# Delta-rule chunks feeding a softplus FFN on one core: loads, one place's matmuls, an inverse's finish and the weight splits moved

## The chip, the cores and the metric

The program runs on one NeuronCore of a Trainium2 chip. The metric is device time in microseconds of one launch. The kernel before was timed three times: 560.78 us is the median, 558.14 the lowest and 563.43 the highest. One more execution was profiled; the profiler puts it at 561.84 us, of which 560.1 us lie between its first and its last instruction (its span). Differences of this kernel under about 1% are not told from no change by a few runs.

## The reference

Attention with the delta rule runs over 32 heads of 768 tokens and 48 channels, token by token. Its outputs, as 3072 rows of 384, go through a two-layer network with a softplus between the layers.

```python
k_n = k / (norm(k, axis=-1) + 1e-06)
for t in range(S):                                  # S = 768
    y[t] = q[t] @ state
    v_old = k_n[t] @ state
    state = state + beta[t] * outer(k_n[t], v[t] - v_old)
x = y.transpose(0, 2, 1, 3).reshape(B * S, H * D)   # 3072 x 384
h = x @ w_in                                        # 384 -> 2048
g = maximum(h, 0) + log1p(exp(-abs(h)))
out = g @ w_out                                     # 2048 -> 384
```

## The kernel before

The 768 tokens are cut into 12 chunks of 64. In a chunk the recurrence becomes a triangular system, whose matrix comes from the products of the keys among themselves (`gram`, L192) and is inverted for two chunks at a time. `invert(u)` does the pair of chunks 2u and 2u+1: for u = 0 on DVE (VectorE), for u = 1 to 5 on POOL (GpSimd) with the lines L338 and L342 in turn. `finish(u)` turns the inverse round with two DVE transposes (L345, L348), and `scale_v` (L146, DVE) scales the values of the pair's first chunk.

Each chunk's output is a piece of x. The FFN takes it in seven passes: chunk 0, chunk 1, then two chunks at a time. A pass of one chunk has 8 *places*, one of two chunks 16, so there are 96 places, t = 0 to 95. At place t the program writes, in this order: `hidden` of t (TensorE, PE: the first layer, L693, for two tiles f = 2g and 2g+1 of 128 hidden units in the passes of one chunk, where g is t within the pass), its Abs, Exp and Ln on ACT (ScalarE, L698 to L700), a helping of the inverse that is running in the background, the blocks of the recurrence that a table `plan` puts at t, the softplus of t on DVE, the weight splits of `LOWS[t]`, `output` of place t-1 (PE, the second layer, L739), the blocks of t + 0.5, and the weight splits of `HIGHS[t]`. Each engine works its own queue in the order written. A helping is as large as due times and a cost table (`costs`, `room`) make it; `END[u]` is the place at which `finish(u)` and `scale_v` enter the background list, and what is due by a place is run off in it.

The pass of chunk 0 multiplies in plain f32 (two records on PE for a matmul), and its softplus is one DVE instruction (L711). From chunk 1 on values go as a high and a low part, three products each: x as x high and x low, the softplus output as `gh` and `gl` (L705, L707, L708 on DVE), the weights as W[f,0] (made by ACT, L666, the table `HIGHS`) and W[f,1] (made by DVE, L670, in `low(f)`, the table `LOWS`). In a trace W[f,1] is the tile a with number f. Place 8+g is the first that uses tiles 2g and 2g+1, so `low(13)` is needed at place 14, as the third of the nine products of f = 13.

Ahead of place 0 stand the loads (all on the SP queue, in the order written), the products of the keys of chunks 0 to 3, the first inverse on DVE, the products `first_p` (L506), and dummy matmuls (`warm`, L815) that nobody reads. The number of columns is their argument; each is two records. Then come `top` and `expand` (ACT L363 and DVE L365), `couple` (L377), `base` (L395), sweeps, `first_u` (DVE L526, ACT L530 and L531) and `first_y`, whose two ACT copies (L548) are the x of place 0. `convert` (DVE L650) joins the two halves of a weight tile.

Of the kernel before, what the change touches and what calls it, by code (L numbers as in the profile page):

```python
# [19 lines left out]
B, H, S, D = 4, 8, 768, 48  # L20
NT, DM, DFF = B * S, H * D, 2048
P = 128
# [4 lines left out]
NK = DM // P  # L27
# [6 lines left out]
ON_ACT = range(2, NS)  # L34
HIGHS = {3: (0,), 4: (1,), 5: (2,), 6: (3, 4), 7: (5, 6), 8: (7, 8, 9), 9: (10, 11),
         10: (12,), 11: (13,), 12: (14, 15)}
LOWS = {5: (0,), 6: (1, 2), 7: (3,), 8: (4, 5, 6), 9: (7,), 10: (8, 9, 10), 11: (11,), 12: (12, 13), 13: (14, 15)}

PASSES = ((0,), (1,), (2, 3), (4, 5), (6, 7), (8, 9), (10, 11))
ROWS, COLS = [[p for p in PASSES if len(p) == k] for k in (1, 2)]  # L40
PASS = {s: i for i, p in enumerate(PASSES) for s in p}

STEPS = {2: (8, 8.5, 9, 9.5, 10.5, 11, 11), 3: (11.5, 12, 13, 13, 13.5, 14, 14)}
CLEAR, DONE, END, GRAM, INV = {}, {1: 8, 2: 19}, {1: 6, 2: 17}, {4: 3.5, 5: 7}, {2: 11}
CLEAR.update({2: 9, 3: 12})
Q_FIRST = (2, 4, 5, 6, 7, 8, 9, 10)
for c in range(4, NS, 2):
    t, u = 8 * (c - 2) + 3, c // 2
# [12 lines left out]
def deltanet_moe(ctx, tc, kT, qT, kI, vN, beta, wts, out, outT):  # L61
    nc = tc.nc
# [13 lines left out]
    def bank(shape):  # L76
        turns[0] += 1
        if turns[0] % 4 == 0 and not both[0]:
            return ps_o.tile(shape, F32, name="po2")
        return ps_a.tile(shape, F32, name="pa")  # L80
# [9 lines left out]
    def hid(shape):  # L90
        t = lent(shape)
        hids[0] += 1
        return t


    tk = [slice(h * C, (h + 1) * C) for h in range(2)]
# [23 lines left out]
    copies = (nc.scalar.copy, nc.vector.tensor_copy)  # L120
# [3 lines left out]
    def load_k(s):  # L124
        kts[s] = KT[s % 4]
        for ab in range(2):
            nc.sync.dma_start(kts[s][dr[ab]], kT[s, ab])

    def load_beta(u):
        bet[u] = two.tile([P, HB], F32, name="bet")  # L130
        nc.sync.dma_start(bet[u], beta[:, u])

    def load_q(s):
        for ab in range(2):
            nc.sync.dma_start(bv[dr[ab], ab, :, 0:C], qT[s, ab])

    def load_ki(s):
        for ab in range(2):
            nc.sync.dma_start(ki[tk[ab], ab], kI[s, tk[ab]])

    def load_v(s):
        NV[s] = two.tile([P, NP, D], F32, name="nv")
        nc.sync.dma_start(NV[s], vN[s])
# [377 lines left out]
    def first_u(g, to):  # L521

        x = x_base[:, 0, 4 * g:4 * g + 4].rearrange("p (b k) c -> p k b c", k=2)
        for ab in range(2):
            t = tk[ab]
            nc.vector.tensor_tensor(still[t, ab, g, 0:2, :, 0:D], x[t],  # L526
                                    to[0][t].rearrange("p (b k) c -> p k b c", k=2), op=ALU.add)
        u = to[1].rearrange("p (b k) c -> p b k c", k=2)
        for ab in range(2):
            nc.scalar.copy(still[tk[ab], ab, g, 2, :, 0:D], u[tk[1 - ab], :, 0])  # L530
            nc.scalar.copy(still[tk[1 - ab], ab, g, :, :, D:],  # L531
                           u[tk[1 - ab], :, 1].rearrange("p b (k c) -> p k b c", k=NK))

# [98 lines left out]
    def top_half(f):  # L632

        t = tops[f % 2].bitcast(F16).rearrange("p (i n w) -> p i n w", i=2, w=2)
        for i, raw in enumerate((RA[f], RB[f])):
            h = raw.bitcast(BF16).rearrange("p (n w) -> p n w", w=4)
            nc.scalar.copy(t[:, i, :, 1], h[:, :, 2])  # L640

    def convert(n=1, parts=(0, 1)):
        for _ in range(n):
            f = done[0]
            if f == done[1]:
                return
            for i in parts:
                words = (RA[f], RB[f])[i].rearrange("p (n w) -> p n w", w=2)
                h = slice(i * DM, (i + 1) * DM)
                nc.vector.scalar_tensor_tensor(RA[f][:, h], words[:, :, 0], 13, tops[f % 2][:, h],  # L650
                                               op0=ALU.logical_shift_right, op1=ALU.bitwise_or)
            if 1 in parts:
                HF[f] = RA[f].bitcast(F32)
                done[0] = f + 1

    def top(n=1):
        for _ in range(n):
            if done[1] in RB:
                assert done[1] < done[0] + 2
                top_half(done[1])  # L660
                done[1] += 1
# [6 lines left out]
    def low(f):  # L668
        W[f, 1] = one.tile([P, 2 * DM], F32R, name=f"a{f}")
        nc.vector.tensor_tensor(W[f, 1], HF[f], W[f, 0], op=ALU.subtract)  # L670


    n = B * C
    PH, A, G, PO = {}, {}, {}, {}

    def weight(i, f, a, c, n):
        return W[f, a][:, c:c + n] if i else HF[f][:, c:c + n]


    def tiles(i, g):  # L680
        return (2 * g, 2 * g + 1) if len(PASSES[i]) == 1 else (g,)

    def hidden(i, g):
        xr = [[X[i][:, k, m].rearrange("p j b t -> p (j b t)") for k in range(NK)]
              for m in range(2 if i else 1)]
        terms = TERMS if i else TERMS[:1]
        fs = tiles(i, g)
        ph = PH[i, g] = hid([P, len(fs), 2 * n // len(fs)])
        for j, f in enumerate(fs):
            c = 0  # L690
            for k in range(NK):
                for a, b in terms:
                    nc.tensor.matmul(ph[:, j], weight(i, f, a, k * P, P), xr[b][k],  # L693
                                     start=(c == 0), stop=(c == len(terms) * NK - 1))
                    c += 1
        ph = PH[i, g] = ph.rearrange("p f t -> p (f t)")
        a = A[i, g] = two.tile([P, 2 * n], F32, name="a")
        nc.scalar.activation(a, ph, AF.Abs)  # L698
        nc.scalar.activation(a, a, AF.Exp, scale=-1.0)  # L699
        nc.scalar.activation(a, a, AF.Ln, bias=1.0)  # L700
# [59 lines left out]
    def run(g):  # L760
        while True:
            try:
                next(g)
            except StopIteration as e:
                return e.value
# [31 lines left out]
    still = one.tile([P, 2, 2, NK, 2, C], F32, name="ot")  # L797
# [12 lines left out]
    def warm(*columns, behind=None):  # L810

        r = even if behind is None else behind
        to = unread[0] if unread else bank([P, 512])
        for m in columns:
            nc.tensor.matmul(to[:, 0:m], even[:, 0:P], r[:, 0:m], start=True, stop=True)  # L815

    with tc.manual_schedule(engines={ET.PE, ET.DVE, ET.Activation, ET.Pool, ET.SP}):
# [7 lines left out]
            nc.gpsimd.memset(bv[pad[ab], ab, :, 0:C], 0.0)  # L825
        load_q(0)
        load_k(2)
        load_v(0)
        load_ki(0)
        load_k(3)  # L830
        load_beta(1)
        feed(4)
        load_v(1)
# [50 lines left out]
        gram(3)  # L884
        pts.append(first_p(1))
        unread.append(bank([P, 512]))
        warm(512, 512)
        run(iv)
        lq = one.tile([P, 2, NP // 2, C], F32, name="ltq")
        MT[0] = [lq[:, 0], lq[:, 1], two.tile([P, NP // 2, C], F32, name="gh")]  # L890
# [15 lines left out]
        def pairs(g):  # L906
            return [(ps_o, ps_h)[g == 0].tile([P, 4, D], F32, name=f"{'po' if g else 'ph'}{e}")
                    for e in range(2)]

        for g in range(2):  # L910
            i, to = slice(4 * g, 4 * g + 4), pairs(g)
# [4 lines left out]
                nc.gpsimd.tensor_copy(x_base[tk[h], 1, i], x_swap[tk[1 - h], i])  # L916
        rest()
        warm(128)
        top()
        for b in range(C // QB):  # L920
            expand(1, b, nc.scalar)
# [11 lines left out]
        for g in range(2):  # L933
            sweep(0, 2, tos[g], 4 * g, 4, ends=(False, True))
            first_u(g, tos[g])
# [3 lines left out]
        load_q(1)  # L939
        load_k(4)  # L940
        load_v(2)
        convert(1, (1,))
        convert()
        rest_of_u()
        top(2)
# [107 lines left out]
        for c in range(2, NS, 2):  # L1053
            u = c // 2
# [8 lines left out]
            for s in (c, c + 1):  # L1063
                a, b, k0, k1, v, y, z = STEPS[s]
# [29 lines left out]
        for t in range(8 * NS):  # L1094
            costs[t] = costs.get(t, 0) + 960 * len(LOWS.get(t, ()))
            costs[t] += 1700 if t > 7 else 2900 if t < 5 else 700
        for i, p in enumerate(PASSES):
            for g in range(NF // 2 * len(p)):
                t = NF // 2 * p[0] + g
                both[0] = both[0] or t >= FOUR  # L1100
                assert done[0] >= 2 * g + 2 or i
                if t < 8 * NS - 1:
                    hidden(i, g)
                if i == 0:
                    convert(2)
                if t == 8 * NS - 2:
                    hidden(i, g + 1)
                over = min(pull(room(t) + over), 0)
                while background and background[0][2] <= t:
                    run(background.pop(0)[0])  # L1110
                for block in plan.pop(t, ()):
                    block()
                softplus(i, g)
                if i == 0:
                    top(2)
                for f in LOWS.get(t, ()):
                    low(f)
                if late:
                    output(*late)
                for block in plan.pop(t + 0.5, ()):  # L1120
                    block()
                for f in HIGHS.get(t, ()):
                    high(f)
                late = i, g
# [61 lines left out]
```

## Time and profile before

| what | value |
|---|---|
| median of three runs | 560.78 us |
| lowest, highest | 558.14, 563.43 us |
| profiled execution, its span | 561.84 us, 560.1 us |
| mean granted clock of TensorE | 0.996 |
| busy: PE, DVE, ACT, POOL | 541.9, 366.9, 363.5, 203.7 us |

Busy time of an engine is the time in which at least one of its instructions runs. A wait is the stretch in which an engine has nothing running, and it is put down to what released it. Times in the rows are microseconds from the start of the span.

### The profile page before, as it was taken

To read this page: it belongs to the slowest core of one execution; us is meant where nothing else is said; L and a number is where in the kernel's file an instruction comes from. 1 tells how busy PE (TensorE), PEld (TensorE's weight loads), DVE (VectorE), ACT (ScalarE), POOL (GpSimd) and SP (SyncE) were. 2 spreads that over 40 slices of the span, in tenths; PEclk is the share of its full clock that TensorE was granted. 3 is DMA by queue.
4 is the path that set the end of the run, shared out by engine and by line. 5 is a ranking of instruction groups with operands and counts; after the bars stand their busy time and mean duration, and the time that the engine had idled before them with its cause. 6 is when DMAs were issued, how large, how long until landed. Compare 5 with 4: busy or idle time off the path is not lost.

```text
span 560.1 us, 17601 instructions
## 1 busy us (share of the span) xinstructions
PE 541.9 (97%) x7477; PEld 445.5 (80%) x7477; DVE 366.9 (66%) x663; ACT 363.5 (65%) x719; POOL 203.7 (36%) x362
## 2 busy tenths in 40 slices
PE   6879999899999999999999999999999999999997
PEld 4567777698987888878888888888888887888885
DVE  7959976999757857368747378747465736444444
ACT  4668877798677864756774757754567754454453
POOL 7122897129970188701886001886000000000000
PEclk9999999899999999999999999999999999999999
DMA  9909913132130122220122320031220020010001
GB/s 209 332 34 334 362 40 69 35 80 67 57 87 4 38 69 60 78 75 4 32 71 59 71 87 3 9 85 31 58 77 4 1 71 2 14 58 1 1 0 57
DMA packets 35502, 39.56 MB, mean 71 GB/s; under 512 B 22528, under 2 KB 25216, under 8 KB 35424
## 3 DMA queue, kind: packets, MB, share of 16 engines
q1 hardware_dynamic: 35280, 38.18, 23.9%
q8 instruction: 59, 0.97, 0.7%
q10 hardware_dynamic: 144, 0.26, 0.1%
q14 instruction: 19, 0.16, 0.1%
HBM read 31.55 MB, written 4.72 MB: 65 GB/s over the span
## 4 chain that ended last, share of the span: by engine, by line
PE 67%; POOL 14%; DVE 5%; issue 2%; ACT 2%; ACTq 0%; DVEq 0%
PE po L739 29%; PE ph L693 27%; POOL Z L342 7%; POOL tmp L338 7%; PE pa L598 3%; PE pa L481 2%; PE pa L441 2%; PE pa L567 1%; DVE tt L348 1%; PE pa L579 1%; PE ph L579 1%; DVE tt L345 1%; PE ph L241 1%; DVE a L705 1%; DVE Z L326 0%
## 5 line engine op out<-in xcount | busy, mean ns | idle before, releaser
L693 PE MATMUL ph<-x,b 128*128 128x512 f32 (+1 forms) x576 | 166.3, 373 | 0.0
L698 ACT ACTIVATE a<-ph 128x512 f32<-128x512 f32 x96 | 57.4, 598 | 155.1 <-PE ph L693 150.5
L693 PE MATMUL ph<-x,a 128*128 128x512 f32 (+1 forms) x384 | 129.5, 375 | 0.6 <-ACT x L548 0.6
L705 DVE SCALAR_TENSOR_TENSOR a<-ph,a 128x512 f32<-128x512 f32 x88 | 60.6, 688 | 94.2 <-ACT a L700 93.8
L693 PEld LDWEIGHTS ph<-x,b 128*128 128x128 f32 x576 | 105.1, 188 | 19.4
L739 PE MATMUL po<-gh,b 128*128 128x512 f32 (+1 forms) x241 | 97.6, 405 | 1.2 <-DVE gh L707 1.2
L342 POOL TENSOR_TENSOR Z<-Z,tmp 128x30 f32<-128x30 f32 (+9 forms) x150 | 89.9, 599 | 11.8
L739 PE MATMUL po<-gh,a 128*128 128x512 f32 (+1 forms) x241 | 94.1, 390 | 0.0
L338 POOL TENSOR_TENSOR tmp<-Z,ltq 128x30 f32<-128x30 f32 (+9 forms) x150 | 86.2, 575 | 11.4
L693 PEld LDWEIGHTS ph<-x,a 128*128 128x128 f32 x384 | 72.0, 189 | 13.2 <-ACT x L548 0.7
L708 DVE TENSOR_TENSOR gl<-a,gh 128x512 fp32r<-128x512 f32 x88 | 66.2, 752 | 7.8 <-DVE gh L707 0.5
L739 PE MATMUL po<-gl,b 128*128 128x512 f32 (+1 forms) x241 | 69.6, 390 | 0.0
L700 ACT ACTIVATE a<-a 128x512 f32<-128x512 f32 x96 | 60.7, 632 | 3.1
L699 ACT ACTIVATE a<-a 128x512 f32<-128x512 f32 x96 | 60.6, 632 | 3.1
L739 PEld LDWEIGHTS po<-gh,b 128*128 128x128 f32 x241 | 45.2, 188 | 12.5 <-DVE gh L707 1.7
L739 PEld LDWEIGHTS po<-gl,b 128*128 128x128 f32 x241 | 45.2, 188 | 10.2 <-DVE gl L708 0.6
L739 PEld LDWEIGHTS po<-gh,a 128*128 128x128 f32 x241 | 45.3, 188 | 8.5
L707 DVE CAST gh<-a 128x512 fp32r<-128x512 f32 x88 | 40.2, 456 | 7.8 <-DVE a L705 0.5
L739 PE MATMUL po<-a,gh 128*128 128x384 f32 x96 | 35.2, 465 | 1.8 <-DVE gh L711 1.8
L604 DVE TENSOR_TENSOR x<-pa,x 128x384 fp32r<-128x384 f32 x20 | 11.1, 555 | 38.0 <-ACT x L603 38.0
L256 POOL COPY ss<-ltq 128x32 f32<-128x32 f32 x6 | 1.5, 244 | 91.6 <-DVE ltq L303 91.6
L495 DVE TENSOR_TENSOR big<-pa,maskP 64x256 f32<-64x256 f32 x66 | 27.8, 420 | 0.9
(222 smaller groups left out, 752.2 us busy)
## 6 DMA issues: line engine op xcount, KB each, us to landing
a<-wts SPq DMA_DIRECT2D x16, 383.8 KB, 7.5
b<-wts SPq DMA_DIRECT2D x16, 383.8 KB, 7.6
kt<-kT SPq DMA_DIRECT2D x24, 192.0 KB, 3.6
big<-qT SPq DMA_DIRECT2D x24, 192.0 KB, 4.1
nv<-vN SPq DMA_DIRECT2D x12, 384.0 KB, 3.4
ki<-kI SPq DMA_DIRECT2D x24, 192.0 KB, 3.3
outT<-ot SPq DMA_DIRECT2D x13, 256.0 KB, 2.2
x<-x SPq DMA_DIRECT2D x66, 32.0 KB, 2.0
```

Of the source, the lines that this page charges most:

```text
L338: engine.tensor_tensor(o, diagonal(Z, blocks, n, j + 1, j, r, j, (True, False)), diagonal(lq, blocks, n, j, 0, r, j, (False, True)), op=AL ...
L342: engine.tensor_tensor(z, z, o, op=ALU.add)
L495: nc.vector.tensor_tensor(be[tk[ab], ab, e, 4 * g:4 * g + 4, 0:C], pks[e][t, :, 0:C], maskP[t].unsqueeze(1).to_broadcast([C, 4, C]), op=AL ...
L598: nc.tensor.matmul(py[tk[ab], i, :], big[:, at + C:at + 2 * C], big[:, at:at + C], start=True, stop=True)
L693: nc.tensor.matmul(ph[:, j], weight(i, f, a, k * P, P), xr[b][k], start=(c == 0), stop=(c == len(terms) * NK - 1))
L698: nc.scalar.activation(a, ph, AF.Abs)
L699: nc.scalar.activation(a, a, AF.Exp, scale=-1.0)
L700: nc.scalar.activation(a, a, AF.Ln, bias=1.0)
L705: nc.vector.scalar_tensor_tensor(a, ph, 0.0, a, op0=ALU.max, op1=ALU.add)
L707: nc.vector.tensor_copy(hi_lo[0], a)
L708: nc.vector.tensor_tensor(hi_lo[1], a, hi_lo[0], op=ALU.subtract)
L739: nc.tensor.matmul(PO[i][h][:, c], l, r, start=(fs[j] == 0 and m == 0), stop=(fs[j] == NF - 1 and m == k - 1 and c != (cut and parts[0])))
```

## The change

Seven edits, in the order of the program:

1. the load of K of chunk 3 stands ahead of V of chunk 0 and of the other layout of K of chunk 0 (`load_ki`) on the SP queue;
2. a third dummy matmul of 512 columns follows the products `first_p(1)`;
3. one DVE conversion (the second half of weight tile 0, L650) is issued ahead of the sweeps and no longer behind `first_u`;
4. one of the eight copies of `first_u` goes from ACT to DVE;
5. place 0 multiplies by token halves: 12 matmuls of 128 columns for 6 of 256, the first six of which need the first copy of x alone;
6. `END[1]` goes from 6 to 7.5: `finish(1)` and its `scale_v` are issued in place 8, behind the softplus and the weight split of place 7;
7. `LOWS`: the splits 6, 9, 11, 13 and 15 are issued one place later, 7 stays in place 9, 10 moves from place 10 to 11, 12 stays at place 12, 14 stays at place 13.

```diff
-LOWS = {5: (0,), 6: (1, 2), 7: (3,), 8: (4, 5, 6), 9: (7,), 10: (8, 9, 10), 11: (11,), 12: (12, 13), 13: (14, 15)}
+LOWS = {5: (0,), 6: (1, 2), 7: (3,), 8: (4, 5), 9: (6, 7), 10: (8,), 11: (9, 10), 12: (11, 12), 13: (13, 14),
+        14: (15,)}
...
-CLEAR, DONE, END, GRAM, INV = {}, {1: 8, 2: 19}, {1: 6, 2: 17}, {4: 3.5, 5: 7}, {2: 11}
+CLEAR, DONE, END, GRAM, INV = {}, {1: 8, 2: 19}, {1: 7.5, 2: 17}, {4: 3.5, 5: 7}, {2: 11}
...
-            nc.scalar.copy(still[tk[ab], ab, g, 2, :, 0:D], u[tk[1 - ab], :, 0])
+            copies[ab * g](still[tk[ab], ab, g, 2, :, 0:D], u[tk[1 - ab], :, 0])
...
-        for j, f in enumerate(fs):
-            c = 0
-            for k in range(NK):
-                for a, b in terms:
-                    nc.tensor.matmul(ph[:, j], weight(i, f, a, k * P, P), xr[b][k],
-                                     start=(c == 0), stop=(c == len(terms) * NK - 1))
-                    c += 1
+        sides = (slice(0, n // 2), slice(n // 2, n)) if i + g == 0 else (slice(0, 2 * n // len(fs)),)
+        for cols in sides:
+            for j, f in enumerate(fs):
+                c = 0
+                for k in range(NK):
+                    for a, b in terms:
+                        nc.tensor.matmul(ph[:, j, cols], weight(i, f, a, k * P, P),
+                                         xr[b][k][:, cols],
+                                         start=(c == 0), stop=(c == len(terms) * NK - 1))
+                        c += 1
...
         load_k(2)
+        load_k(3)
         load_v(0)
         load_ki(0)
-        load_k(3)
...
-        warm(512, 512)
+        warm(512, 512, 512)
...
         warm(128)
+        convert(1, (1,))
         top()
...
-        convert(1, (1,))
         convert()
```

How the order of instructions moves is shown at three places. First the SP queue at the start, where kt_76 and kt_77 are K of chunks 2 and 3, nv the values of chunk 0 and ki the other layout of its K. Before:

```order
L127 DMA kt_76<-kT 48x1024 x2
L143 DMA nv<-vN 128x768
L139 DMA ki<-kI 64x768 x2
L127 DMA kt_77<-kT 48x1024 x2
L131 DMA bet<-beta 128x32
```

and now:

```order
L128 DMA kt_76<-kT 48x1024 x2
L128 DMA kt_77<-kT 48x1024 x2
L144 DMA nv<-vN 128x768
L140 DMA ki<-kI 64x768 x2
L132 DMA bet<-beta 128x32
```

K of chunk 3 has moved past three transfers; nothing else moves on this queue.

Second, DVE around places 7 and 8. gh_1563 (gh_1566 in the change) is the softplus output of place 7, the L345, L348 and L146 are the finish of inverse 1, a_1594 (a_1597) is the softplus of place 8, and a3 to a6 are weight splits. Before:

```order
L345 STREAM_TRANSPOSE tt_1517<-Z_80 128x32x32
L348 STREAM_TRANSPOSE tt_1517<-Z_80 128x32x32
L146 TENSOR_TENSOR nv_765<-nv_765,nn_839 128x768
L711 SCALAR_TENSOR_TENSOR gh_1563<-ph1_1506,a_1513 128x512
L670 TENSOR_TENSOR a3_1565<-a4_130,b3_1502 128x768
L705 SCALAR_TENSOR_TENSOR a_1594<-ph0_1575,a_1594 128x512
```

and now:

```order
L715 SCALAR_TENSOR_TENSOR gh_1566<-ph1_1513,a_1520 128x512
L671 TENSOR_TENSOR a3_1568<-a4_130,b3_1509 128x768
L346 STREAM_TRANSPOSE tt_1601<-Z_80 128x32x32
L349 STREAM_TRANSPOSE tt_1601<-Z_80 128x32x32
L147 TENSOR_TENSOR nv_767<-nv_767,nn_846 128x768
L709 SCALAR_TENSOR_TENSOR a_1597<-ph0_1578,a_1597 128x512
```

The softplus of place 7 and the split 3 now stand ahead of the finish; the lines of the change are one to four higher in number.

Third, DVE in place 13: the masks of the keys (L495), the softplus of place 13, and the splits behind it. Before:

```order
L495 TENSOR_TENSOR big_78<-pa_2260,maskP_81 64x4x64 x2
L495 TENSOR_TENSOR big_78<-pa_2261,maskP_81 64x4x64 x2
L495 TENSOR_TENSOR big_78<-pa_2280,maskP_81 64x4x64 x2
L495 TENSOR_TENSOR big_78<-po2_2281,maskP_81 64x4x64 x2
L705 SCALAR_TENSOR_TENSOR a_2256<-ph1_2237,a_2256 128x512
L707 CAST gh_2311<-a_2256 128x512
L708 TENSOR_TENSOR gl_2312<-a_2256,gh_2311 128x512
L670 TENSOR_TENSOR a14_2315<-a15_810,b14_2233 128x768
L670 TENSOR_TENSOR a15_2317<-a16_814,b15_2235 128x768
```

and now:

```order
L496 TENSOR_TENSOR big_78<-pa_2265,maskP_81 64x4x64 x2
L496 TENSOR_TENSOR big_78<-pa_2266,maskP_81 64x4x64 x2
L496 TENSOR_TENSOR big_78<-pa_2285,maskP_81 64x4x64 x2
L496 TENSOR_TENSOR big_78<-po2_2286,maskP_81 64x4x64 x2
L709 SCALAR_TENSOR_TENSOR a_2261<-ph1_2242,a_2261 128x512
L711 CAST gh_2316<-a_2261 128x512
L712 TENSOR_TENSOR gl_2317<-a_2261,gh_2316 128x512
L671 TENSOR_TENSOR a13_2320<-a14_807,b13_2150 128x768
L671 TENSOR_TENSOR a14_2322<-a15_811,b14_2238 128x768
```

The split 13, which stood a place earlier, now follows the softplus of place 13, and place 14 is the one that uses it.

## Rows read from the trace of the kernel before

**Rows 1.** The page: busy us, share of the span, instructions of each engine.
```profile
PE 541.9 (97%) x7477; PEld 445.5 (80%) x7477; DVE 366.9 (66%) x663; ACT 363.5 (65%) x719; POOL 203.7 (36%) x362
```
**Rows 2.** Waits of PE: line and releaser, total us, times, longest us.
```profile
PE po L395 <- issue: 2.1, 2, 1.6
PE po L739 <- DVE gh L711: 1.8, 2, 1.4
PE pa L418 <- DVE x L606: 0.9, 1, 0.9
PE ph L693 <- ACT x L548: 0.6, 1, 0.6
```
**Rows 3.** Timeline of SP and PE, 7 to 32 us: start, us, instruction [idle before, releaser].
```profile
9.97 2.25 SPq L127 DMA_DIRECT2D kt<-kT  x2
...
19.10 0.87 PE L192 MATMUL po<-kt 48*64 48x64 f32 x3 [2.47 <-DMA kt<-kT]
22.96 3.78 PE L815 MATMUL pa<-gl 128*128 128x512 f32 x4
27.76 0.27 PE L377 MATMUL pa<-tt,x 64*64 64x64 f32 x2
...
31.23 0.55 PE L395 MATMUL po<-nv,tt 64*64 64x48 f32 x19 [1.63 <-issue]
```
**Rows 4.** DMA engines, 8 to 20 and then 22 to 31.3 us: packets, and GB/s in 40 slices.
```profile
DMA packets 2364, 2.68 MB, mean 223 GB/s; under 512 B 1679, under 2 KB 1679, under 8 KB 2363
...
GB/s 423 423 410 410 396 423 431 409 383 396 409 396 409 409 423 396 423 423 409 423 423 423 409 423 409 409 409 396 225 163 106 66 53 53 53 48 0 0 0 0
```
**Rows 5.** Timeline of ACT and DVE ahead of place 0 and in it.
```profile
25.47 0.91 ACT L363 ACTIVATE tt<-tmp,blk 128x256 f32<-128x256 f32 x2 [0.90 <-DVE nn L279]
37.42 0.24 ACT L530 COPY ot<-ph 64x96 f32<-64x96 f32 x1 [3.66 <-PE ph L395]
...
48.84 0.69 DVE L711 SCALAR_TENSOR_TENSOR gh<-ph,a 128x512 f32<-128x512 f32 x1
```
**Rows 6.** Timeline of DVE, ACT and PE at places 7 and 8.
```profile
95.95 2.00 DVE L345 STREAM_TRANSPOSE tt<-Z 128x1024 f32<-128x1024 f32 x1 [4.63 <-POOL Z L342]
...
100.52 0.71 DVE L711 SCALAR_TENSOR_TENSOR gh<-ph,a 128x512 f32<-128x512 f32 x1
101.98 0.72 DVE L705 SCALAR_TENSOR_TENSOR a<-ph,a 128x512 f32<-128x512 f32 x1
...
100.64 0.63 ACT L700 ACTIVATE a<-a 128x512 f32<-128x512 f32 x1
...
94.19 2.85 PE L739 MATMUL po<-a,gh 128*128 128x384 f32 x8
101.29 4.54 PE L739 MATMUL po<-a,gh 128*128 128x384 f32 x8 [1.42 <-DVE gh L711]
```
**Rows 7.** Windows: bounds, length, busy of PE, PEld, DVE, ACT, POOL, granted clock, DMA.
```profile
102.00:105.40 3.40, 3.40 (x7) 1.67 (x5) 3.30 (x6) 1.19 (x3) 0.00 (x0) 0.51 0.13 50
130.00:140.00 10.00, 10.00 (x179) 9.19 (x177) 9.59 (x17) 9.67 (x17) 9.14 (x12) 1.00 0.31 80
```
**Rows 8.** Timeline of DVE and PE, places 12 to 15.
```profile
134.68 2.56 DVE L670 TENSOR_TENSOR a<-a,b 128x768 fp32r<-128x768 f32 x2
141.77 0.69 DVE L705 SCALAR_TENSOR_TENSOR a<-ph,a 128x512 f32<-128x512 f32 x1
143.91 2.75 DVE L670 TENSOR_TENSOR a<-a,b 128x768 fp32r<-128x768 f32 x2
149.08 1.03 DVE L708 TENSOR_TENSOR gl<-a,gh 128x512 fp32r<-128x512 f32 x1
...
141.17 0.50 PE L693 MATMUL ph<-x,b 128*128 128x256 f32 x2
143.30 0.28 PE L693 MATMUL ph<-x,a 128*128 128x256 f32 x1
149.15 0.40 PE L693 MATMUL ph<-x,b 128*128 128x256 f32 x2
```

## The prediction

> **What bounds the kernel now.** The page comes first: PE is busy for 541.9 of 560.1 us [rows 1], so the time is PE's work plus the little that PE waits or runs slowly. The list of PE's waits comes second [rows 2]. It is short, and the timeline puts all of it ahead of 150 us: there the edits lie too. From 150 us on PE works through, and a microsecond that it is early or late at place 16 is one at the end. So I follow one number, PE's lead over the kernel before, from the start to place 16.
>
> Three stretches make up the early loss. At the start PE waits 2.47 us for K of chunk 3 before the products of its keys, and 1.63 us in `base`, where no semaphore is to blame [rows 3]. At places 7 and 8 it waits 1.42 us for the softplus L711, which stands on DVE behind the finish of the inverse. That finish can't start before POOL ends at 95.95 [rows 6]. After this wait the granted clock falls to 0.51 for 3.4 us, its lower level of 1.2 GHz [rows 7], and the eight records of L739 take 4.54 us, where the same eight took 2.85 a little earlier [rows 6]. The third stretch shows in a window: between 130 and 140 us PE is busy for all of the 10 us, but DVE for 9.59 too [rows 7]. There the two engines run level, and what PE gains ahead of it is kept only if DVE comes along.
>
> **The start (edits 1 to 5).** The load of K of chunk 3 is issued at 9.97 behind 384 KB of values and 192 KB of the other layout. At the 223 GB/s that the DMA engines moved from 8 to 20 us [rows 4] these 576 KB are 2.6 us, so the load lands about that much earlier, and the wait of 2.47 us goes, nearly whole. The two transfers it passes land later; their readers come after 26 us, so I price that at nothing (cover: some 8 us; without it POOL's scaling of the values would be late by up to 1 us). The third dummy adds two records of 3.78/4 = 0.95 us, 1.9 us in all, on the same queue [rows 3]. That leaves 0.6 us at `couple` if the records stay this slow. `couple` can't start before ACT's `expand` ends at 25.47 + 0.91 = 26.38 [rows 5], so at most 27.76 - 26.38 = 1.4 us is to be had. I take 0.9.
>
> The pause of 1.63 us ends at 31.23 without a releaser [rows 3]. Until about 28.5 us the DMA engines are full at some 410 GB/s, then they fall idle [rows 4], and PE goes on 2.7 us later. I read it as PE's next instructions, fetched late behind data. The change brings PE into the block before earlier by the 2.5 us of the load, while `base` starts at most 1.4 us earlier, so the fetch has a longer run; I take 1.6 us gained, bounds 0 and 1.6. The Trainium skill speaks against this reading ("Runtime: NRT & Kernel Launch", section "Instruction fetch mechanics"): the sequencer fetches the next block on its own DMA queue while it executes the present one, and crossing a block is mostly hidden. By that rule the 1.63 us has another cause, nothing of it is won, and the sum is 1.6 us higher; it is rival C's ground.
>
> The copy that goes from ACT to DVE takes 0.24 us off ACT's row of eight copies ahead of the x of place 0 [rows 5]; DVE has room there: 0.2 us gained. The earlier conversion only takes DVE time from behind `first_u` to a place where DVE idles: 0, with 0.5 as its bound either way. The token halves at place 0 can win no more than PE's wait of 0.6 us for the second copy of x [rows 2]. They win less, as the output of place 0 waits for L711 at 48.84 [rows 5], which is late on DVE (the 0.4 us left of that wait's 1.8 [rows 2]): 0, bounds -0.6 and +0.6, since twice as many weight loads do the same columns. Sum of the start: 0.9 + 1.6 + 0.2 = 2.7; I take 2.5, as PE's lead is partly spent at place 0 on that softplus. Bounds: 0 and 3.6.
>
> **Places 7 and 8 (edit 6).** L711 of place 7 now stands ahead of the finish, in the 4.63 us for which DVE idles before 95.95 [rows 6]. The wait of 1.42 us goes, and with it the slow stretch of 4.54 - 2.85 = 1.69 us: 3.1 us gained, bounds 0 and 3.1. The finish still starts when POOL ends, so its readers at place 8 get it no later. What is queued behind the finish now is L705 of place 8: it started at 101.98 and can't start before its own a, which ACT ends at 100.64 + 0.63 = 101.27 [rows 6]. So DVE wins only 0.7 us here, PE 3.1. PE's lead is 2.5 + 3.1 = 5.6 us, DVE's 3.2.
>
> **Splits 9, 11, 13 and 15 (edit 7).** Each now stands behind a softplus in the place just ahead of its use. In the kernel before, the split 13 was done at 137.2, while PE began the place that uses it at 141.17 [rows 8]: 4 us to spare. Now it stands behind the softplus of place 13, L705 at 141.77. What moves that L705: DVE's lead of 3.2 us, and one split fewer ahead of it, 2.56/2 = 1.3 us; less some 0.9 us that PE's own waits for splits 9 and 11 and for L606 [rows 2] hand back to DVE through ACT. That is 3.6 us, so L705 starts at 138.2. The splits follow 143.91 - 141.77 = 2.14 us later, and one takes 2.75/2 = 1.4 us [rows 8]: split 13 is done at 141.7. PE, with its whole lead, would want it at 141.17 - 5.6 + 11 x 0.125 = 137.0 (it is for the twelfth of 18 records, which stand (143.30 - 141.17)/17 = 0.125 us apart). So PE stands 4.7 us in all over places 12 to 14, the most of it at 14. Seven records remain, and the first layer of place 14 ends at 142.6, where it ended at 143.6: 1.0 us of the lead is left.
>
> Split 15 then follows the softplus of place 14, whose last part L708 ends at 149.08 + 1.03 = 150.1, now 1.0 us earlier. With the split it is done at 150.5, and PE wants it at 149.15 - 1.0 + 1.4 = 149.6 [rows 8]. That takes 0.9 us more. Net: 2.5 + 3.1 - 4.6 - 0.9 = 0.1 us gained. The number hangs on DVE: the start's bounds go through it one to one, the 0.9 handed back may be 0.2 to 1.6, and a split 1.0 to 1.4 us.
>
> **The sum.** 561.84 - 0.1 = 561.7 for the profiled execution, which stands 1.06 above the median of the runs; against the median that is 560.6 us. The own range of this case is 558.5 to 562.0.
>
> **Rivals.** A, *the splits come in time*. DVE idles for 0.4 us in ten where it is fullest [rows 7], and the waits that I hand back to it may not arise; splits run at 1.0 us where POOL is quiet. For it: DVE's own queue gets shorter ahead of each late split. Against it: 13 needs DVE to be 4.7 us earlier than I find it. With all of it kept: 561.84 - 5.6 = 556.2, against the median 555.2; with half, 558. Chance 0.17.
>
> B, *the clock falls at the new wait*, the side that is slower. A wait of 1.42 us was followed by the fall at 102 us [rows 6, 7]; the one of 0.87 us for L606 [rows 2] by none (the clock is 1.00 in the window behind it [rows 7]). My wait at place 14 is longer than the first. Each fall costs what the other did, 1.69 us, unless PE then has less to wait for split 15. It decides from a single wait of about 1.4 us: one fall gives 560.6 + 1.7 = 562.3, two 564.0, which is slower than before. Against it: the one fall seen followed a stretch with lighter records as well. The Trainium skill has the general rule ("TensorE: Matmul & The Clock Gate", Part 1): the throttled clock is the default, and activity releases it; the row at 102 us agrees. Chance 0.25.
>
> C, *the start does not do what it says*: the load lands earlier, but the pause ends when the data end, at 31.2, and the third dummy eats the rest. The 1.6 us of the start are then missing on DVE and PE alike: 560.6 + 1.6 = 562.2. Chance 0.13. The main case has 0.45.
>
> **Range and chances.** One per cent, 5.6 us, is what a measurement here tells from no change: faster means below 555.2, slower above 566.4. Only A's better half reaches the first, with a little for gains I don't see: 0.11. The second needs two falls and a lost start: 0.04. Within 1%: 0.85. The range runs from 556.5 to 563.5; A's better half and two falls are left out.
>
> **What would show it.** `Couple` about 1 us earlier and no pause without a releaser in `base`; L739 of place 7 in 2.9 us at full clock; PE's waits list with L693 waiting for DVE's a (L671 in the new numbering) at places 12 to 15, the longest at 14 and over 2 us; PE some 5 us early at place 10 and level at place 16. Wrong, if those waits are missing (A), or if the granted clock dips near 140 us (B).

## The result: 0.7% slower, and the profile after

The changed kernel takes 564.58 us (median of ten runs, 563.19 to 566.67), the kernel before 560.96 beside it. The ratio is 1.0068, its interval 1.0045 to 1.009. I had forecast 560.6 us and no change. The profiled execution of the change has a span of 563.8 us, 3.7 more than the one before. Medians and ratios, here and below, leave out two runs far above the rest: 601.82 us in run 12 and 2972.15 us of the kernel before.

PE's waits, as line and releaser, total us, times, longest us:

```profile
PE ph L696 <- DVE a L671: 5.2, 3, 2.7
PE po L507 <- issue: 2.9, 1, 2.9
...
PE po L743 <- DVE gh L711: 1.2, 2, 0.6
PE po L743 <- DVE gh L715: 0.8, 1, 0.8
...
PE po L396 <- issue: 0.5, 1, 0.5
```

Of the two pauses in `base` of [rows 2] the one of 1.6 us is gone and the other, of 0.5, is still there; the 1.42 us for the softplus of place 7 and the 0.87 us for the x of L606 (the low part of a chunk's output, made by DVE) are gone. The wait for the softplus of place 0 has grown from 0.3 to 0.8 us (L715). Two lines are new: 5.2 us for weight splits (L671 is `low`) and 2.9 us without a releaser in `first_p`. The timeline has the places where they stand, beside the loads:

```profile
5.49 2.85 SPq L128 DMA_DIRECT2D kt<-kT  x4
...
22.16 0.49 PE L507 MATMUL po<-big,kt 48*64 48x64 f32 x9 [2.85 <-issue]
22.58 5.24 PE L819 MATMUL pa<-gl 128*128 128x512 f32 x6
...
28.72 0.27 PE L378 MATMUL pa<-tt,x 64*64 64x64 f32 x2
```

Against [rows 3], the wait for K of chunk 3 is gone and the dummies start 0.4 us earlier (22.58 for 22.96), not 2.5: PE stands for 2.85 us before the last nine records of `first_p`. The third dummy's two records then bring `couple` to 28.72, 1.0 us later than before. Without the pause in `base` PE is 1.2 to 1.3 us early at places 0 and 1, and 0.8 from place 2 to place 8, after the longer wait for the softplus of place 0.

Places 7 and 8 went as forecast. DVE and PE there:

```profile
94.35 0.69 DVE L715 SCALAR_TENSOR_TENSOR gh<-ph,a 128x512 f32<-128x512 f32 x1 [3.84 <-ACT a L704]
...
95.83 2.04 DVE L346 STREAM_TRANSPOSE tt<-Z 128x1024 f32<-128x1024 f32 x1
...
100.49 0.69 DVE L709 SCALAR_TENSOR_TENSOR a<-ph,a 128x512 f32<-128x512 f32 x1
...
98.99 2.85 PE L743 MATMUL po<-a,gh 128*128 128x384 f32 x8
...
102.61 0.51 PE L696 MATMUL ph<-x,b 128*128 128x256 f32 x2
```

The eight records take 2.85 us where [rows 6] had 1.42 of wait and 4.54. Place 9 begins at 102.61, for 106.44 before: 3.8 us early. Then come the splits, on DVE and on PE:

```profile
140.59 0.69 DVE L709 SCALAR_TENSOR_TENSOR a<-ph,a 128x512 f32<-128x512 f32 x1
...
142.87 2.69 DVE L671 TENSOR_TENSOR a<-a,b 128x768 fp32r<-128x768 f32 x2
...
127.14 0.39 PE L696 MATMUL ph<-x,a 128*128 128x256 f32 x1 [1.35 <-DVE a L671]
...
133.63 0.39 PE L696 MATMUL ph<-x,a 128*128 128x256 f32 x1 [1.13 <-DVE a L671]
...
144.29 0.58 PE L696 MATMUL ph<-x,a 128*128 128x256 f32 x1 [2.70 <-DVE a L671]
...
151.44 0.44 PE L743 MATMUL po<-b,gh 128*128 128x384 f32 x1
...
153.65 0.40 PE L696 MATMUL ph<-x,b 128*128 128x256 f32 x2
```

PE waits for splits 9, 11 and 13, the last time for 2.70 us. Place 15 begins at 153.65, for 149.15 before [rows 8]: 4.5 us late. The windows around place 14 (length, then busy of PE, PEld, DVE, ACT, POOL, granted clock, DMA) say why the loss exceeds the wait:

```profile
143.00:144.20 1.20, 0.00 (x0) 0.00 (x0) 1.20 (x1) 0.00 (x0) 1.12 (x2) 0.71 0.00 0
144.20:147.60 3.40, 3.31 (x35) 3.09 (x37) 1.32 (x2) 1.35 (x3) 3.08 (x5) 0.50 0.02 5
147.60:151.00 3.40, 3.40 (x92) 3.40 (x90) 1.24 (x4) 1.96 (x6) 3.08 (x5) 0.60 0.00 0
151.00:152.00 1.00, 1.00 (x27) 0.95 (x22) 0.96 (x4) 0.96 (x3) 0.85 (x2) 1.00 0.00 0
```

The clock falls to its lower level during the wait and comes back only at 150.3. Some 7 us pass at half speed, 0.8 of them in the wait: twice the stretch of [rows 7]. This is rival B, and its price is higher than I gave it.

### The profile page after: what moved, and what is told of

Its sections match the earlier page's. It is cut to its first block, busy times and chain, and to the rows that moved or that the text cites. A ratio compares the mean times of both kernels' runs of the same rounds, so it can differ in the third digit from the quotient of the medians.

```text
span 563.8 us, 17622 instructions
## 1 busy us (share of the span) xinstructions
PE 544.3 (97%) x7491; PEld 448.6 (80%) x7491; DVE 367.5 (65%) x664; ACT 363.0 (64%) x718; POOL 202.6 (36%) x362
## 4 chain that ended last, share of the span: by engine, by line
PE 86%; DVE 8%; ACT 4%; issue 1%; ACTq 0%; DVEq 0%
PE po L743 33%; PE ph L696 33%; PE pa L599 4%; PE pa L482 3%; PE pa L819 2%; PE pa L442 2%; PE pa L568 1%; PE pa L580 1%; PE pa L193 1%; DVE a L671 1%; DVE a L709 1%; PE ph L580 1%; DVE big L496 1%; PE ph L242 1%; DVE gl L712 1%
## 5 line engine op out<-in xcount | busy, mean ns | idle before, releaser
L696 PE MATMUL ph<-x,a 128*128 128x512 f32 (+2 forms) x396 | 130.4, 370 | 5.2 <-DVE a L671 5.2
L709 DVE SCALAR_TENSOR_TENSOR a<-ph,a 128x512 f32<-128x512 f32 x88 | 60.5, 688 | 96.5 <-ACT a L704 96.1
L743 PE MATMUL po<-a,gh 128*128 128x384 f32 x96 | 33.5, 444 | 0.8 <-DVE gh L715 0.8
```

Of the source, the lines that this page charges most:

```text
L696: nc.tensor.matmul(ph[:, j, cols], weight(i, f, a, k * P, P), xr[b][k][:, cols], start=(c == 0), stop=(c == len(terms) * NK - 1))
L709: nc.vector.scalar_tensor_tensor(a, ph, 0.0, a, op0=ALU.max, op1=ALU.add)
L743: nc.tensor.matmul(PO[i][h][:, c], l, r, start=(fs[j] == 0 and m == 0), stop=(fs[j] == NF - 1 and m == k - 1 and c != (cut and parts[0])))
```

## The experiments

Medians are of 6 to 12 runs; each ratio is against runs of the kernel before on the same chip. "Early" and "late" compare the starts of the same PE instructions with the profiled execution before. Line numbers shift by a few from kernel to kernel: `hidden` is L693 to L699, `output` L739 to L746, `low` L670 or L671.

**1. The splits back at their places.** The change with the old table:

```diff
-LOWS = {5: (0,), 6: (1, 2), 7: (3,), 8: (4, 5), 9: (6, 7), 10: (8,), 11: (9, 10), 12: (11, 12), 13: (13, 14), 14: (15,)}
+LOWS = {5: (0,), 6: (1, 2), 7: (3,), 8: (4, 5, 6), 9: (7,), 10: (8, 9, 10), 11: (11,), 12: (12, 13), 13: (14, 15)}
```

> The change with the weight splits at their places of before; the other six edits stay. Theory (the splits issued one place before use make PE wait at places 12 to 15, and the longest wait takes the clock down): the three waits of L693 for the splits (5.2 us) and the half-clock stretch near 144 us are gone; PE keeps the lead of some 3.8 us that it has at place 9, less about 0.5 to 1: 557 us, ratio 0.993 to 0.996 against before. Rival (the start or the finish behind the softplus cost the time, the splits hardly): still above before, 562 to 564 us, ratio 1.003 to 1.006.

559.97 us, ratio 0.9985 (0.9968 to 1.0003). The loss is gone: edit 7 costs 564.58 - 559.97 = 4.6 us within the change. But the gain that I expected is not there either. PE's wait and the window behind it in this run:

```profile
124.21 0.75 PE L418 MATMUL pa<-tt,off 32*32 32x32 f32 x64 [1.98 <-DVE x L606]
...
124.80:128.20 3.40, 3.40 (x33) 3.36 (x20) 3.33 (x5) 2.33 (x5) 3.08 (x5) 0.50 0.13 31
```

PE, 4.4 us early at place 9, waits 1.98 us for the x of L606, where it waited 0.87, and the clock falls there. At place 13 it is 1.9 us early. DVE is the bound of this stretch even with the splits in time.

**2. Split 13 alone back.**

```diff
-12: (11, 12), 13: (13, 14), 14: (15,)}
+12: (11, 12, 13), 13: (14,), 14: (15,)}
```

> The change with split 13 alone back at place 12 (ahead of the softplus of place 13); 9, 11 and 15 stay late. Theory: the wait of 2.7 us at place 14 and the half-clock stretch behind it go, the waits of about 1.3, 1.1 and 0.5 us for splits 9, 11 and 15 stay, and the clock stays at 1.00: 558.5 to 559.5 us, ratio 0.995 to 0.998. Rival (any of the waits takes the clock down, or all four splits cost alike): two of three waits and a fall remain, 562 us or more, ratio 1.002 to 1.005.

561.21 us, ratio 1.0005 (0.9989 to 1.0022). This one split carries 564.58 - 561.21 = 3.4 of the 4.6 us, the other late ones 1.2. Its profile has three waits for splits left, 3.2 us together, and no fall behind any; the windows that held the fall:

```profile
PE ph L696 <- DVE a L671: 3.2, 3, 1.4
...
140.00:150.00 10.00, 10.00 (x212) 9.61 (x204) 8.99 (x15) 6.73 (x15) 9.06 (x13) 1.00 0.15 49
```

The time is above the range that I gave: PE, 3.3 us early at place 9 in this profile, loses all but 0.4 by the end, and the three waits make 3.2.

**3. The wait filled with work.** The change, with 22 dummies before the products of f = 13 at place 14; their result is overwritten.

```diff
             for j, f in enumerate(fs):
                 c = 0
+                for _ in range(22 if i == 1 and f == 13 else 0):
+                    nc.tensor.matmul(ph[:, j, cols], weight(i, f, 0, 0, P), xr[0][0][:, cols],
+                                     start=True, stop=True)
```

> The change, with 22 dummy matmuls (128x256, nobody reads their result) at place 14 ahead of the products of f = 13, where PE otherwise waits for split 13: some 2.6 us of work in a wait of 2.7 us. Theory (the price of that place is in two parts, the wait and the fall of the clock that it causes): the first layer of place 14 ends when it did, within 0.3 us, no half-clock stretch follows, and some 3 us come back: 561 to 562 us, ratio 1.000 to 1.003. Rival (the clock falls for another reason, or costs nothing beside the wait): 564 to 565 us, ratio 1.006 to 1.009.

563.57 us, ratio 1.0053 (1.0035 to 1.0072), 1.0 us under the change. The profile does what the theory says:

```profile
140.93 2.80 PE L695 MATMUL ph<-x,b 128*128 128x256 f32 x22
144.05 0.39 PE L699 MATMUL ph<-x,a 128*128 128x256 f32 x1
145.08 1.15 PE L599 MATMUL pa<-big 128*64 128x64 f32 x32
152.71 0.39 PE L699 MATMUL ph<-x,a 128*128 128x256 f32 x1 [0.52 <-DVE a L671]
...
140.00:150.00 10.00, 9.92 (x176) 9.52 (x176) 7.48 (x12) 6.35 (x15) 9.14 (x12) 1.00 0.16 43
```

Split 13 arrives as late as before (144.05), but the clock stays at 1.00 and the y products of L599 take 1.15 us for 1.98 in the change. PE is 2.9 us earlier than the change at the products behind; a part goes at once, since it now waits 0.52 us for split 15. So the wait and the fall are two prices, and the fall's is 1 us in the median, 2.0 in the profiled spans (563.8 and 561.8; 0.3 of it is an earlier start). I had forecast some 3 us.

**4. The late splits on the kernel before.** Only `LOWS` as in the change.

```diff
-LOWS = {..., 8: (4, 5, 6), 9: (7,), 10: (8, 9, 10), 11: (11,), 12: (12, 13), 13: (14, 15)}
+LOWS = {..., 8: (4, 5), 9: (6, 7), 10: (8,), 11: (9, 10), 12: (11, 12), 13: (13, 14), 14: (15,)}
```

> The kernel before with the late weight splits alone. Theory: PE waits some 2.5 us at place 14 for split 13, 0.5 to 1.3 us for 9, 11 and 15, the clock falls near 145 us as well as near 102 us: 2.9 us for the waits and some 3 for the fall, 566 to 568 us, ratio 1.008 to 1.013. Rival (the late splits only cost where the other edits bring PE ahead of DVE): PE comes no earlier than the splits, 561 to 562 us, ratio 1.000 to 1.003.

566.45 us, ratio 1.0099 (1.0069 to 1.013): edit 7 costs 5.5 us by itself, so it needs no early PE to do harm. Three rows of this run, the waits, place 7's `output`, and a window behind place 14:

```profile
PE ph L694 <- DVE a L671: 5.2, 3, 2.7
...
101.67 2.85 PE L740 MATMUL po<-a,gh 128*128 128x384 f32 x8 [1.39 <-DVE gh L712]
...
148.20:151.60 3.40, 3.40 (x75) 3.40 (x70) 0.76 (x2) 2.38 (x7) 3.01 (x6) 0.50 0.02 5
```

The waits are the same 5.2 and 2.7 us as in the change. And a second thing: the 1.39 us wait at place 7 is there, but the clock doesn't fall behind it; the eight records take 2.85 us. The same wait has the fall of [rows 7] in some executions and not in others (run 6 has it again).

**5. Edit 6 alone.**

```diff
-CLEAR, DONE, END, GRAM, INV = {}, {1: 8, 2: 19}, {1: 6, 2: 17}, {4: 3.5, 5: 7}, {2: 11}
+CLEAR, DONE, END, GRAM, INV = {}, {1: 8, 2: 19}, {1: 7.5, 2: 17}, {4: 3.5, 5: 7}, {2: 11}
```

> The kernel before with edit 6 alone: the finish of inverse 1 behind the softplus and the split of place 7. Theory (the softplus no longer stands behind the finish): the wait of 1.42 us at 99.9 us and the fall of the clock behind it are gone, 1.4 to 3.1 us; of it up to 1 us is lost again at place 11, where PE then waits longer for the x of L606: 558.5 to 560 us, ratio 0.995 to 0.998. Rival (the readers of the finish come late instead): a wait at place 8 takes its place, 561 us, ratio 0.999 to 1.003.

560.21 us, ratio 0.9979 (0.996 to 0.9998): 0.8 us. In its profile PE waits nowhere from 98 to 110 us, then 2.0 us for L606 and a fall behind that, as in run 1:

```profile
98.00:110.00 12.00, 12.00 (x241) 9.71 (x240) 11.76 (x18) 11.62 (x25) 1.53 (x2) 1.00 0.11 37
126.00:129.40 3.40, 3.40 (x18) 3.35 (x16) 3.33 (x5) 2.12 (x5) 3.09 (x5) 0.50 0.16 39
```

**6. The five edits at the start alone.** The change with `END` and `LOWS` of before.

```diff
-LOWS = {..., 8: (4, 5), 9: (6, 7), 10: (8,), 11: (9, 10), 12: (11, 12), 13: (13, 14), 14: (15,)}
+LOWS = {..., 8: (4, 5, 6), 9: (7,), 10: (8, 9, 10), 11: (11,), 12: (12, 13), 13: (14, 15)}
...
-... {1: 8, 2: 19}, {1: 7.5, 2: 17}, ...
+... {1: 8, 2: 19}, {1: 6, 2: 17}, ...
```

> The change without edits 6 and 7, that is the five edits at the start alone. Theory (the wait for K of chunk 3 hid a wait for PE's next instructions of nearly the same length, and the third dummy adds 1.5 us): the wait for K goes, a pause of 2.5 to 3 us in the first_p products takes its place, the pause in base goes: 0.5 to 1.3 us won, 560 us, ratio 0.997 to 1.000. Rival (the start won its 2.5 us and lost them only at the late splits): 558 to 558.5 us, ratio 0.995.

559.56 us, ratio 0.9974 (0.9957 to 0.9992). The gain is 1.5 us by the medians, 1.2 us of lead in the profile, and the 2.5 us of my sum are not to be had. The wait for K has become a pause without a releaser. At place 7, where the finish is again as before, the wait and the slow eight records of [rows 6] are back:

```profile
PE po L506 <- issue: 2.4, 1, 2.4
...
100.09 4.54 PE L742 MATMUL po<-a,gh 128*128 128x384 f32 x8 [1.42 <-DVE gh L714]
```

**7. The splits spread out.** The change, with split 10 alone later than before, and two dummies.

```diff
-8: (4, 5), 9: (6, 7), 10: (8,), 11: (9, 10), 12: (11, 12), 13: (13, 14), 14: (15,)}
+8: (4, 5, 6), 9: (7,), 10: (8, 9), 11: (10, 11), 12: (12, 13), 13: (14, 15)}
...
-        warm(512, 512, 512)
+        warm(512, 512)
```

> The change with the weight splits evenly ahead of their use (8: 4 5 6, 9: 7, 10: 8 9, 11: 10 11, 12: 12 13, 13: 14 15, so split 10 alone stands a place later than before) and with two dummies of 512 columns in place of three. Theory: no wait for a split, the wait for the x of L606 at place 11 is 0.9 us and no longer 2.0, and the start is 0.8 to 1.7 us earlier than with three: 557 to 558.5 us, ratio 0.993 to 0.996. Rival (DVE is the bound up to place 16 whatever the order of the splits): as with the splits of before, 560 us, ratio 0.998.

560.54 us, ratio 0.9982 (0.9962 to 1.0001): the rival. The waits for splits and for L606 are gone, and another took their place, up to 1.7 us for the masks of the keys. Behind it the profiled execution has a stretch of 6.8 us at half clock, so this time isn't that of the order of the splits alone:

```profile
PE pa L567 <- DVE big L495: 2.3, 2, 1.7
...
137.50:144.20 6.70, 6.25 (x82) 5.97 (x84) 6.48 (x10) 2.04 (x5) 6.07 (x9) 0.50 0.21 59
```

**8. The loads held back.** Run 7's kernel, its next weights and the values of chunk 1 loaded after the first inverse. They wait for a memset of one column of the tile that the first of them fills.

```diff
-        feed(4)
-        load_v(1)
-        feed(6)
...
         run(iv)
+        feed(4, True)      # first: nc.vector.memset(t.bitcast(F32)[:, 0:1], 0.0)
+        load_v(1)
+        feed(6)
```

> The kernel of the run before this one in this list, with the loads of the next weights and of the values of chunk 1 (3 MB) held back until the first inverse is done (some 24.5 us; a memset of one column of the first weight tile is what they wait for). Theory (PE's instructions come late because their fetch shares the DMA engines with these loads): the pause of 2.5 to 3 us in the first_p products is under 0.5 us, PE is 1 to 2 us earlier at couple: 556 to 557.5 us, ratio 0.990 to 0.994, unless the weights then come late for place 1. Rival (the pause has nothing to do with the data): the pause stays, and the time is that of the run before or longer, ratio 0.994 to 1.000.

564.95 us, ratio 1.0068 (1.0046 to 1.0091). The timeline of PE, 18 to 40 us, the longest waits, and three windows (the last number is the DMA engines' GB/s):

```profile
20.09 0.49 PE L506 MATMUL po<-big,kt 48*64 48x64 f32 x9 [0.39 <-issue]
31.34 0.55 PE L395 MATMUL po<-nv,tt 64*64 64x48 f32 x19 [3.26 <-issue]
37.79 0.26 PE L395 MATMUL po<-x,ltq 64*64 64x48 f32 x2 [1.69 <-issue]
...
18.00:20.00 2.00, 1.71 (x64) 1.56 (x57) 1.76 (x8) 1.95 (x6) 0.00 (x0) 0.50 0.02 5
28.00:31.00 3.00, 0.08 (x5) 0.00 (x0) 0.52 (x2) 2.76 (x7) 0.68 (x2) 1.00 0.96 334
32.70:36.00 3.30, 3.30 (x90) 2.70 (x82) 1.72 (x6) 0.00 (x0) 0.58 (x1) 0.50 1.04 413
```

The change, in the pause of its `first_p`:

```profile
20.00:22.00 2.00, 0.00 (x0) 0.00 (x0) 1.79 (x7) 1.89 (x6) 0.00 (x0) 1.00 1.01 398
```

The theory's step is confirmed and its price missed. With the DMA engines idle (5 GB/s for 398), the same nine records of `first_p` pause for 0.39 us, not 2.85, and end 2 us earlier. But the held loads then run through `base` and the sweeps, and the pauses come back there, longer (3.26 and 1.69 us), with a half-clock stretch behind the first. The pause follows the data.

**9. The load alone.**

```diff
         load_k(2)
+        load_k(3)
         load_v(0)
         load_ki(0)
-        load_k(3)
```

> The kernel before with edit 1 alone: K of chunk 3 loaded ahead of the values. Theory (behind the wait for K stands the arrival of PE's instructions): the wait of 2.5 us at the products of chunk 3's keys goes, a pause of 2 to 2.9 us in first_p takes its place, and without the third dummy PE is 0 to 0.8 us earlier at couple; with the pause in base smaller, 0.5 to 1.5 us at place 0: 559.5 to 560.5 us, ratio 0.997 to 0.999. Rival (the load is what made the start late): 2.5 us, 558.5 us, ratio 0.995.

560.08 us, ratio 0.9988 (0.9974 to 1.0002). Its pause, beside the shorter one in `base`:

```profile
22.21 0.50 PE L506 MATMUL po<-big,kt 48*64 48x64 f32 x9 [2.68 <-issue]
30.55 0.55 PE L395 MATMUL po<-nv,tt 64*64 64x48 f32 x19 [0.47 <-issue]
```

`first_p` ends at 22.21 + 0.50 = 22.7 us here, at the same time in the change, and with K late it ended at 23.0, where the dummies of [rows 3] begin. Two things set that moment, and the load was only one of them.

**10. Two dummies for three**, with the splits of before and the rest of the change.

```diff
-        warm(512, 512, 512)
+        warm(512, 512)
```

> The change with the weight splits at their places of before and with two dummies of 512 columns in place of three. Theory (the third dummy lies on PE's way to couple, 0.43 to 0.85 us a record): 0.5 to 1.5 us under the run with the splits back and three dummies (559.97 us), so 558.5 to 559.5 us, ratio 0.996 to 0.998. Rival (the third dummy keeps the clock up and pays for itself): 560 us or more, ratio 0.998 to 1.001.

559.49 us, ratio 0.9977 (0.9965 to 0.9989), against run 1's 559.97: 0.5 us, within what these runs vary. The profile shows where the dummy's time goes: PE is at `couple` at 26.68 us, for 27.71 in run 1, and then pauses longer in `base`. Run 10, then run 1:

```profile
30.35 0.55 PE L395 MATMUL po<-nv,tt 64*64 64x48 f32 x19 [1.84 <-issue]
...
30.24 0.56 PE L395 MATMUL po<-nv,tt 64*64 64x48 f32 x21 [0.70 <-issue]
```

**11. Place 11 filled.** Run 10's kernel, with twelve dummies where PE waits for L606.

```diff
+        def fill(k):
+            to, x = lent([P, 512]), X[1][:, 0, 0].rearrange("p j b t -> p (j b t)")
+            for _ in range(k):
+                nc.tensor.matmul(to[:, 0:n], W[0, 0][:, 0:P], x, start=True, stop=True)
+
+        at(11.5, 0, bind(fill, 12))
```

> The kernel of the run before this one in this list, with 12 dummy matmuls (128x256, 1.44 us of work, nobody reads them) at place 11, where PE waits 2.0 us for the x of L606. Theory (a wait of about 2 us is followed by a fall of the clock in most runs, and it is the fall that eats what edit 6 brings): no half-clock stretch near 125 us in the profile, PE goes on at the same time as without the dummies, 1 to 1.6 us faster: 557.5 to 558.5 us, ratio 0.994 to 0.996. Rival (the fall near 125 us was chance): no difference to the run before, ratio 0.996 to 0.998.

559.14 us, ratio 0.9964 (0.9951 to 0.9978), the fastest version found. The wait is filled and the clock stays up:

```profile
123.34 1.59 PE L1059 MATMUL ph<-x,b 128*128 128x256 f32 x12
125.46 0.74 PE L418 MATMUL pa<-tt,off 32*32 32x32 f32 x64 [0.54 <-DVE x L606]
...
120.00:130.00 10.00, 9.46 (x229) 9.02 (x226) 9.79 (x15) 6.85 (x17) 8.90 (x16) 1.00 0.25 52
```

Against run 10 it is 0.35 us, less than forecast, and the intervals overlap: that the dummies pay is not shown.

**12. The start alone, with two dummies.**

```diff
-        warm(512, 512, 512)
+        warm(512, 512)
```

> The five edits at the start with two dummies of 512 columns in place of three; finish and splits as before. Theory: 0.5 to 1.5 us under the run with three (559.56 us): 558 to 559 us, ratio 0.994 to 0.997. Rival (the third dummy pays for itself): 559.5 to 560.5 us, ratio 0.997 to 0.999.

559.76 us, ratio 0.9986 (0.997 to 1.0002), against 559.56 with three. Runs 10 and 12 differ in sign, so what the third dummy costs or brings is below what these runs tell.

## Why the prediction was wrong

The mechanism of edit 7 was right in every link: the waits stand for splits 9, 11 and 13 at the places named, the longest at place 14. Run 1 shows that they carry the loss, run 2 that split 13 carries most of it. The likeliest case failed in two terms of its sum: the start, taken at 2.5 us, gave PE 0.8, and the half clock at place 14, which the sum had at nothing, took 3.0. The other terms came near: 3.0 us at places 7 and 8 for 3.1, and 5.2 us of waits for splits for 4.7 + 0.9.

**The start, 2.5 us.** I took the wait for K of chunk 3 as the thing to remove and asked only what PE does with the time. Next in line stood PE's own instructions. I had named their late arrival, for `base`, and had not asked where the same thing waits once PE is early in `first_p`. Runs 6 and 9 show the pause there, run 8 that it belongs to the data traffic. `Couple` came 1.0 us late where I had it 0.9 early; the 1.6 us of `base` came, and 0.8 us of the 2.5 was left behind place 0. One profile is a rough measure of this: at place 2 PE is 0.4 us late in run 4 and 0.55 early in run 5, both with the start of before, and 0.35 to 1.3 early with the five edits. Rival C was nearer than its chance of 0.13: the pause in `base` went in the change because PE came there later. In runs 1, 6, 9, 10 and 11 it is there again, 0.5 to 2.0 us long, and ends at 30.2 to 30.7 us, 0.5 to 1.0 before that of [rows 3]. The Trainium skill's rule that crossing a block of instructions is mostly hidden ("Runtime: NRT & Kernel Launch", "Instruction fetch mechanics") fits run 8's 0.39 us with idle DMA engines; with full ones the measured 2.85 us decides. That these pauses are the fetch of instructions is the reading that fits runs 6, 8 and 9. No row names their cause, but in all 14 profiles each of them ends 2.2 to 3.0 us after a 16 KB packet of the DMA queue that the profile calls instruction. In the change it is this one between 19 and 20 us, begun at 19.6; PE goes on at 22.16:

```profile
q8 instruction: 1, 0.02, 6.3%
```

**Split 13, done at 141.7.** It was done at 144.2. L709 started at 140.59, where I had 138.2: the 1.7 us that the start lacked went straight through DVE, as the prediction said they would, and some 0.7 more came from DVE's waits. PE, with less lead and two waits behind it, wanted the split later too, so its waits in all came near the sum, 2.70 us of them in one piece.

**The clock.** I gave the fall at place 14 a chance of 0.25, as a rival. A wait of 1.42 us had been followed by one, and my own sum held a longer wait; by the rows the fall was the likelier course. None of the change's ten runs has a mean clock above 0.997, and none of its profile's shorter waits, 1.35 and 1.13 us, had a fall behind it. The stretch behind the third was 6.8 us in the profiled execution (143.5 to 150.3), two times that of [rows 7]; I had priced it at one. Between the starts of places 14 and 15 PE goes from 1.2 us early to 4.5 late: 2.70 us are the wait and 3.0 the half clock. Behind place 19 0.7 us comes back, so PE ends 3.7 late. Run 3 shows the fall as a cost of its own.

**Places 7 and 8, 3.1 us.** This came in the profile, 3.0 us of lead, but 1.69 of it stood against an execution of the kernel before that had a fall there. Run 4 and run 9 have the same wait without it, run 6 with it. Of the 28 executions of the kernel before beside runs 1 to 4, 13 have a mean clock of at least 0.994 (the profiles with a lower mean all have half-clock stretches on record in the first 43 us, so their mean says nothing of place 7): seven of these have 0.998 or more and a median of 559.67 us, six have less and 561.64. So what the median gains by removing that fall is a part of 1.69; run 5 measured 0.8 us for edit 6 in all, its later wait for L606 included.

The token halves, the earlier conversion and the moved copy were priced near nothing. With edits 1 and 2 they make 1.5 us (run 6); apart from the load (run 9: 0.7 us by its ratio, 1.0 by the medians, and its interval reaches no change) nothing of them is told from none.

## What to carry to other kernels

Before pricing a removed wait, list what else the engine needs at the same moment, its own instructions among it, and let the next latest one set the gain. In a stretch where two engines run level, work moved to just before its use on the busier one makes the other wait for it, ahead or not (4.6 us here with the other edits, 5.5 without). And a wait on TensorE that may take the clock down is two prices: look at several executions before counting a fall that a change removes as time won, and count it as likely where the change adds a wait longer than one that was followed by a fall.

## What the runs showed of the hardware

The wait of 1.4 us on PE at place 7 was followed by a fall of the granted clock in two profiled executions (before and run 6) and by none in two others (runs 4 and 9); that of 1.7 us for the masks by one in run 7 and none in run 8; waits of 2.0 and 2.7 us by one in runs 1, 4, 5 and 10 and in the change. The stretch at half clock was 3.4 us or 6.8. Work with no use in the wait prevented it in the profiles of runs 3 and 11. PE's pauses without a releaser at the start were up to 3.3 us long, each behind a packet of the instruction queue; the one in `first_p` was 0.4 us where the DMA engines were idle and 2.2 to 3.1 where they were full. A mean clock near 1 doesn't say that the start ran at full clock: the profile before lists 1.00 there, yet 31 records of L177 at 7.8 us take 1.16 us, and 0.68 in run 1, where its clock is 1.00 too.
